# Output products of 512 columns for ten of sixteen granules, with the halves added by VectorE

## The chip, the core and the metric

The kernel runs on one core of one Trainium2 chip. The metric is the device time of one launch in microseconds. A comparison uses the median of several runs; the profile is one further execution, recorded by the hardware profiler.

## What is computed

The output is `x + A(xn) + B(xn)`, where `xn` is the layer norm of `x` (2048 tokens of 1024 columns, bfloat16). `A` is attention with a recurrent memory: the tokens are cut into 64 segments of 32, and each segment attends over itself and 8 memory rows that the segment before it produced.

```
for s in range(n_seg):                       # 64 segments, one after another
    h = concat([mem, x[s]])                  # 8 memory rows + 32 tokens
    q, k, v = h @ Wq, h @ Wk, h @ Wv         # 32 heads of 128
    p = softmax(mask(q k^T * scale))
    o = (p v) @ Wo                           # 40 rows of 1024
    mem, out[s] = o[:8], o[8:]
```

`B` picks the two tokens with the highest router score, sends them through a gated feed-forward network and adds the result to these two rows. It makes up the last part of the program and is not touched.

## The kernel before, in words

**Main rows and left rows.** The memory of a segment depends on the segment before it, so the segments are a strict sequence. Of a segment's 32 tokens, the first 24 ("main" rows) go with the 8 memory rows as 32 rows through the products of that segment. The last 8 tokens ("left" rows) of four segments are gathered into another 32 rows per group of four segments (`G, j = divmod(s, 4)`), whose products (`left_pass` at L579, `project_left` at L598) are spread over the group as fillers, at places written out by hand in `PASSES`.

**Granules.** The four weight matrices are cut into 64 granules of 128 partitions x 2048 columns (512 KB). Granules 0 to 47 are Wq, Wk and Wv in six phases of eight (`PHASES`), granules 48 to 63 are Wo, each with the rows of two heads: an even head in its columns 0 to 1023, an odd one in 1024 to 2047. 44 granules stay in SBUF. The other 20 (`STREAMED`) are loaded in each segment again, by SyncE (`fetch`, L366), from a copy in DRAM (`wsc`) into five slots (`N_SLOT`). A slot's next load is issued as soon as TensorE has done with its granule (`after`, called by `release`). Granule 6 is kept whole in PSUM instead, and of granule 25 a half. The kept pieces of granule 6 are copied back to SBUF once in a segment by `bring_back` (L389): pieces 1 and 2 after output granule 9, piece 1 by ScalarE and piece 2 by VectorE; pieces 3 and 0 at the beginning of the next segment.

**Phases.** In each of the phases 0 to 5 of a segment a granule makes four products of 512 columns (L817): the stationary operand is a chunk of 32 columns of `ST` (the normalized main rows and the memory rows, transposed), and the four products go to the four groups of 32 partitions of one PSUM bank. The sums are copied out, transposed and used for scores, softmax and attention by functions that `hook` places at a phase and granule.

**The output stage** (called phase 6) takes the 16 granules of Wo. `project` (L586) makes for each of a granule's two heads four products of 256 columns, product `g` with the columns `256 g` and on to partitions `32 g` to `32 g + 31`, columns 0 to 255 of the bank `WO`. Columns 256 to 415 of the same bank hold sums of the attention of half 0 until ScalarE has copied them (L745, L747). Attention of half 1 is called ahead of granules 5 and 8 (`attend(1, 0)`, `attend(1, 1)`); its results are copied by ScalarE (first product group) and VectorE (second), to `OT` for the main rows and `OTL` for the left rows. After granule 15 VectorE adds `WO` to `X[s % 2]`, the residual rows in the same layout (L885), POOL sends out the rows (L887), and the memory rows are transposed into the next segment's `ST` (`mem_to_st`: L301 on TensorE, L324 on VectorE). With these the next segment's phase 0 can begin. `run_passes(7, 0)` and `run_passes(8, 0)` put left passes of TensorE into that gap.

**Names that matter for the change.** `psA` has two PSUM banks with the tag "acc", for the six `PSm` of a segment and for `WO`, in turn. `roles` is a list of three SBUF tags of 1024 bytes per partition that rotates once in a group; `roles[0]` is the one that is free for short tenants: `XBl` (sums of the left rows' q and k, copied by `copy_unit` at L627 and stored to `ql_d` by a DMA that ScalarE issues, L628), `BX` and `XL` (left rows and zeros), and piece 0 of granule 6 (`BK`). In segments 1 and 2 of a group the second of two such stores is issued behind the copy of phase 5's sums (L846). A tile that takes over a tag waits until everything that used the tile before it is done, its DMAs too. Every engine works off its instructions in order.

**Order of columns.** `X`, the memory rows and the output use blocks of 256 columns, block `g` on partitions `32 g`. The left rows' output already uses products of 512 columns and the crossed order `2 * (g % 2) + g // 2`, and adds its halves in `copy_unit` (L616, L619).

Of the kernel before, what the change touches and what calls it, by code (L numbers as in the profile page):

```python
# [9 lines left out]
F32 = mybir.dt.float32  # L10
U32 = mybir.dt.uint32
ALU = mybir.AluOpType
# [4 lines left out]

N_RES = 44
N_SLOT = 5
KEPT_WHOLE = 6  # L20
KEPT_PART = 25
NEG = -30000.0
# [28 lines left out]
def kernel(  # L51
# [16 lines left out]
    nc = tc.nc  # L68
# [204 lines left out]
    def two_rows(m, tag):  # L273
# [52 lines left out]
    def load_left(G, t, crossed=False):  # L326

        o4 = x2[4 * G * SEG:4 * (G + 1) * SEG, :].rearrange("(s r) d -> s r d", s=4)[:, XM:SEG, :]
        if not crossed:
            o4 = o4.rearrange("s r d -> r s d")  # L330
        for g in range(4):
            b = 2 * (g % 2) + g // 2 if crossed else g
            nc.gpsimd.dma_start(out=t[32 * g:32 * (g + 1), :], in_=o4[:, :, 256 * b:256 * (b + 1)])
        return t

# [33 lines left out]
    def part(t, jq):  # L369
        return t[jq][:, :] if isinstance(t, list) else t[:, 512 * jq:512 * (jq + 1)]  # L370
# [16 lines left out]
    def bring_back(c, copy):  # L387
        back[c] = one.tile([P, 512], BF16, tag=(roles[0], "bE", "kt", "bC")[c], name="BK")
        copy(out=back[c][:, :], in_=KEPT_COLS[KEPT_WHOLE][c])  # L389

# [45 lines left out]
    OB = one.tile([P, 256], BF16, tag="bA", name="MEM0")  # L436
    nc.vector.memset(OB[:, :], 0.0)
    for g in range(4):
        nc.gpsimd.dma_start(out=OB[32 * g + XM:32 * g + SEG, :], in_=A_mem0[0, :, 256 * g:256 * (g + 1)])
    n_x = 1  # L440
    n_q = 0
    for g in range(48):
# [99 lines left out]
    def passes_of(s):  # L542
        out = {}
        for at, ps in places[s % 4].items():
            for u, g in ps:
                if not 0 <= group_of(u, s) < NT:
                    continue
                if s == 0:
                    after_first.append((u, g))
                elif s == NSEG - 1 and u == "o":  # L550
                    pass
                else:
                    out.setdefault(at, []).append((u, g))
        if s == 1:
            out.setdefault((0, 7), []).extend(after_first)
        if s == NSEG - 1:
            for w in range(16):
                out.setdefault((6, max(w, 3)), []).append(("o", 48 + w))
        return out
# [19 lines left out]
            nc.tensor.matmul(PSl[32 * jq:32 * jq + 32, :], lhsT=STL[:, g % KC, :], rhs=part(Gv, jq),  # L579
                             start=first_, stop=last_, tile_position=(0, 32 * jq))  # L580

    def project(PS, w, Gv, lhs, last, first=False):
        for hs in range(2):
            h = 2 * w + hs
            for g in range(4):
                nc.tensor.matmul(PS[32 * g:32 * g + 32, 0:256], lhsT=lhs(h),  # L586
                                 rhs=Gv[:, D * hs + 256 * g:D * hs + 256 * (g + 1)], start=(first and hs == 0),
                                 stop=(last and hs == 1), tile_position=(0, 32 * g), skip_group_check=True)

    xl_of, otl_of = [None], [None]  # L590

# [9 lines left out]
    def copy_unit(u, s, engine):  # L601
        PS, n = units.pop(u)
        assert n == 0, (u, s, n)
        Gu = group_of(u, s)
        copy = nc.scalar.copy if engine == "scalar" else nc.vector.tensor_copy
        half = int(u[-1]) if u != "o" else 0
        if u[0] == "v":
            new_vl[half] = one.tile([P, 512], BF16, tag=roles[half], name="VL")
            copy(out=new_vl[half][:, :], in_=PS[:, :])
            if half:  # L610
                roles.insert(0, roles.pop())
        elif u == "o":
            OL = xl_of[0]
            LF = one.tile([P, 256], F32, tag="otl", name="LF")
            for c in range(2):
                nc.scalar.copy(out=LF[64 * c:64 * c + 64, :], in_=PS[64 - 64 * c:128 - 64 * c, 256 * c:256 * c + 256])  # L616
            for c in range(2):
                here = slice(64 * c, 64 * c + 64)
                nc.vector.tensor_tensor(out=LF[here, :], in0=PS[here, 256 * c:256 * c + 256], in1=LF[here, :], op=ALU.add)  # L619
            nc.gpsimd.tensor_tensor(out=OL[:, :], in0=LF[:, :], in1=OL[:, :], op=ALU.add)  # L620
            o4 = out2[4 * Gu * SEG:4 * (Gu + 1) * SEG, :].rearrange("(s r) d -> s r d", s=4)
            for g in range(4):
                b = 2 * (g % 2) + g // 2
                nc.gpsimd.dma_start(out=o4[:, XM:SEG, 256 * b:256 * (b + 1)], in_=OL[32 * g:32 * (g + 1), :])
        else:
            XBl = one.tile([P, 512], BF16, tag=roles[0], name="XBl")
            copy(out=XBl[:, :], in_=PS[:, :])  # L627
            stores.append(lambda: nc.scalar.dma_start(out=ql_d[Gu][2 * half + "qk".index(u[0])], in_=XBl[:, :]))  # L628
            if engine == "scalar":
                stores.pop()()  # L630

    for s in range(NSEG):
# [91 lines left out]
        def attend(half, ph, turn_too=None):  # L724
            if half not in sums:
                if half not in OT:
                    OT[half] = one.tile([P, 4, 4, SEG], BF16, tag=("kt", "bC")[half], name="OT")
                if half == 0:
                    nxt["wo"] = psA.tile([P, 512], F32, tag="acc", name="WO")
                sums[half] = [BS[:, 0:4 * NK] if half else nxt["wo"][:, 256:256 + 4 * NK], OPB]  # L730
            PTm, PTl = PTs[half]
            for il in range(4):
                for jl in range(2):
                    q0 = 32 * (2 * ph + jl)
                    o = sums[half][jl][:, il * NK:(il + 1) * NK]
                    nc.tensor.matmul(o, lhsT=VM[half][q0:q0 + 32, il * P:(il + 1) * P], rhs=PTm[q0:q0 + 32, il, 0:NK],  # L736
                                     start=True, stop=False, tile_position=(q0, 0), skip_group_check=True)
                    nc.tensor.matmul(o, lhsT=VL[half][q0:q0 + 32, il * P:(il + 1) * P], rhs=PTl[q0:q0 + 32, il, 0:NK],
                                     start=False, stop=True, tile_position=(q0, 0), skip_group_check=True)
            if turn_too is not None:  # L740
                turn_too()
            for jl in range(2):
                ov = sums[half][jl].rearrange("p (i q) -> p i q", i=4)
                copy = nc.scalar.copy if half == 0 or jl == 0 else nc.vector.tensor_copy
                copy(out=OT[half][:, 2 * ph + jl, :, :], in_=ov[:, :, 0:SEG])  # L745
                h0 = 16 * half + 8 * ph + 4 * jl
                copy(out=left_out()[:, h0:h0 + 4, j, :], in_=ov[:, :, SEG:NK])  # L747
# [61 lines left out]
        for p, (mat, half) in enumerate(PHASES):  # L809
# [3 lines left out]
            for kc in range(KC):  # L813
                g = 8 * p + kc
                Gv = back if s > 0 and g == KEPT_WHOLE else granule(g)
                for jq in range(4):
                    nc.tensor.matmul(PSm[32 * jq:32 * jq + 32, :], lhsT=ST[:, kc, :], rhs=part(Gv, jq),  # L817
                                     start=(kc == 0), stop=(kc == KC - 1), tile_position=(0, 32 * jq))
                if g in KEPT_COLS and s == 0:
                    keep(g, Gv)  # L820
                if s > 0:
                    held[g] = Gv
                    run_passes(p, kc)
                    release(p, kc)
                else:
                    behind.append((g, Gv))
                    if kc >= 3 or p == 0:
                        for g_, Gv_ in behind:
                            left_pass(PSl, g_, Gv_, g_ % KC == 0, g_ % KC == KC - 1)
                            after(s, g_)  # L830
                        behind = []
                for fn in hooks.pop((p, kc), []):
                    fn()
# [30 lines left out]
        for w in range(16):  # L864
# [18 lines left out]
            release(6, w)  # L883
        OB = X[s % 2]
        nc.vector.tensor_tensor(out=OB[:, :], in0=WO[:, 0:256], in1=OB[:, :], op=ALU.add)  # L885
        for g in range(4):
            nc.gpsimd.dma_start(out=out2[s * SEG:s * SEG + XM, 256 * g:256 * (g + 1)], in_=OB[32 * g:32 * g + XM, :])  # L887
        run_passes(7, 0)
        if s + 1 < NSEG:
            mem_to_st(OB, nxt["st"])  # L890
# [123 lines left out]
```

## Time and profile before

| | |
|---|---|
| median of 3 runs | 1869.23 us (1857.4 to 1875.79) |
| time of the profiled execution | 1871.21 us |
| its span, first to last instruction | 1869.1 us |
| mean granted TensorE clock | 0.957 |
| TensorE products of L586 | 8192 matmuls, 8192 weight loads |
| TensorE products of L817 | 12288 matmuls |
| bytes moved by DMA | 712.27 MB, 381 GB/s in the mean |

How to read the profile: PE is TensorE's matmuls, PEld its weight loads, DVE VectorE, ACT ScalarE, POOL GpSimd, SP SyncE. A line of the groups names the kernel line, the engine, the operation, the tile written and those read, the shape, the count, the busy time, the mean duration in ns, and the idle time of the engine just ahead of it with what ended that. In the order of time a row begins with its start and its length in us; a count behind it says how many instructions follow each other in it, and brackets give the idle time ahead. In the chain of waits each row is a start, a length and what the chain passes through. A table by stage gives for each engine busy time and count, then the granted clock, the share of the 16 DMA engines and GB/s. The last row of an answer on one line gives its DMAs' time from issue to landing.

### The profile page before, as it was taken

How to read it: one execution, taken by the hardware profiler on the slowest of the kernel's cores; microseconds unless marked ns; L12 is line 12 of the kernel's file. 1: busy time of each engine (PE TensorE's matmuls, PEld its weight loads, DVE VectorE, ACT ScalarE, POOL GpSimd, SP SyncE). 2: the span in 40 equal slices, each digit the busy share in tenths (PEclk: the TensorE clock that was granted, in tenths of full speed). 3: DMA queues.
4: the chain of work that ended last, by engine and by line, in shares of the span. 5: the costliest groups of instructions: out<-in, count | busy, mean ns of one | idle time of the engine just before them, and what ended most of it. 6: DMA issues, size and time to landing. Idle time of an engine off the chain costs nothing.

```text
span 1869.1 us, 80529 instructions
## 1 busy us (share of the span) xinstructions
PE 1568.8 (84%) x34978; PEld 847.9 (45%) x34978; DVE 896.9 (48%) x2950; ACT 683.6 (37%) x1933; POOL 457.1 (24%) x898
## 2 busy tenths in 40 slices
PE   3458998898998988888899988988889988988764
PEld 1124444444444444444444444444445544444433
DVE  6725544554455444544554455544544455445430
ACT  1113433444343433434344334434334343433320
POOL 3111322213231322223132322323132221312220
PEclk8669999999999999999999999999999999999995
DMA  9999999999999999999999999999999999999998
GB/s 370 406 355 373 388 386 380 393 382 387 394 385 392 366 383 391 359 380 385 388 375 388 389 384 387 373 396 374 378 369 396 394 382 383 378 377 352 384 402 338
DMA packets 230322, 712.27 MB, mean 381 GB/s; under 512 B 39040, under 2 KB 52912, under 8 KB 229968
## 3 DMA queue, kind: packets, MB, share of 16 engines
q1 hardware_dynamic: 192592, 671.18, 93.0%
q0 software_dynamic: 28736, 28.08, 4.7%
q10 hardware_dynamic: 8640, 7.87, 1.2%
q8 instruction: 274, 4.49, 0.9%
q14 instruction: 80, 0.66, 0.1%
HBM read 694.32 MB, written 22.29 MB: 383 GB/s over the span
## 4 chain that ended last, share of the span: by engine, by line
DMA 61%; PE 32%; DVE 4%; issue 1%; ACT 1%; SPq 0%; ACTq 0%; DVEq 0%
DMA g<-wsc 54%; PE PSm L817 17%; PE WO L586 4%; PE PSl L579 4%; PE BT L649 2%; DMA XP<-in_A_x_dram 2%; PE WL L598 1%; DMA MW<-in_B_w_gate_dram 1%; DVE XR L256 1%; DMA MW<-in_B_w_up_dram 1%; DMA g<-in_A_Wq_dram 1%; DMA wres<-in_A_Wo_dram 1%; DMA g<-in_A_Wo_dram 1%; DMA MW<-in_B_w_down_dram 1%; DMA g<-in_B_w_down_dram 1%
## 5 line engine op out<-in xcount | busy, mean ns | idle before, releaser
L817 PE MATMUL PSm<-wres,ST 128*32 128x512 bf16 x8448 | 700.5, 383 | 6.5 <-DMA wres<-in_A_Wv_dram 3.5
L817 PEld LDWEIGHTS <-ST 128*32 128x32 bf16 x12288 | 323.6, 96 | 412.7 <-issue 168.2
L817 PE MATMUL PSm<-g,ST 128*32 128x512 bf16 x3588 | 360.0, 386 | 97.7 <-DMA g<-wsc 76.3
L586 PEld LDWEIGHTS <-OT 128*32 128x32 bf16 x8192 | 217.6, 97 | 166.6 <-issue 141.0
L836 ACT CAST XB<-PSm 128x512 bf16<-128x512 f32 x256 | 150.7, 589 | 283.9 <-PE PSm L817 280.8
L586 PE MATMUL WO<-wres,OT 128*32 128x256 bf16 x5632 | 237.6, 278 | 12.3 <-DMA wres<-in_A_Wo_dram 8.0
L495 POOL DMA_DIRECT2D LX<-ql_d x63 | 35.4, 562 | 814.0 <-PE WO L586 423.2
L586 PE MATMUL WO<-g,OT 128*32 128x256 bf16 x2560 | 133.3, 281 | 84.1 <-DMA g<-wsc 72.6
L579 PE MATMUL PSl<-wres,STL 128*32 128x512 bf16 x2112 | 184.5, 390 | 0.4 <-issue 0.4
L887 POOL DMA_DIRECT2D out_dram<-X x256 | 130.2, 515 | 211.9 <-DVE X L885 169.4
L664 DVE COPY KT<-BT 128x512 bf16<-128x512 bf16 x112 | 45.9, 410 | 278.7 <-issue 121.8
L281 POOL DMA_DIRECT2D X<-in_A_x_dram x256 | 130.1, 515 | 179.6 <-PE PSm L817 88.8
L389 ACT COPY BK<-KEPT 128x512 bf16<-128x512 bf16 x126 | 74.3, 590 | 131.2 <-PE WO L586 99.8
L657 ACT COPY QT<-BT 128x512 bf16<-128x512 bf16 x128 | 75.0, 586 | 127.1 <-PE BT L502 78.1
L649 PEld LDWEIGHTS <-XB 128*128 128x128 bf16 x1024 | 58.6, 98 | 117.1 <-ACT XB L836 75.2
L885 DVE TENSOR_TENSOR X<-WO,X 128x256 bf16<-128x256 f32 x64 | 27.2, 425 | 172.3 <-PE WO L586 172.3
L649 PE MATMUL BT<-IDENT,XB 128*128 128x128 bf16 x1024 | 102.2, 223 | 8.2 <-ACT XB L836 6.7
L579 PEld LDWEIGHTS <-STL 128*32 128x32 bf16 x3072 | 84.0, 98 | 53.0 <-issue 8.5
L846 ACT CAST VM<-PSm 128x512 bf16<-128x512 f32 x128 | 76.5, 598 | 83.3 <-PE PSm L817 82.8
L736 PEld LDWEIGHTS <-VM 32*128 32x128 bf16 x2048 | 65.1, 91 | 83.7 <-issue 72.7
L393 DVE COPY g<-KEPT 128x512 bf16<-128x512 bf16 x126 | 47.6, 420 | 101.7 <-PE PSm L817 51.5
L681 DVE TENSOR_TENSOR BS<-BS,CT 128x96 f32<-128x96 f32 (+1 forms) x256 | 59.1, 231 | 72.8 <-PE BS L674 68.3
(175 smaller groups left out, 2371.9 us busy)
## 6 DMA issues: line engine op xcount, KB each, us to landing
g<-wsc SPq DMA_DIRECT2D x1134, 512.0 KB, 6.0
g<-wsc SPq DMA_DIRECT2D x63, 256.0 KB, 5.7
LX<-ql_d POOLq DMA_DIRECT2D x63, 128.0 KB, 5.6
ql_d<-XBl ACTq DMA_DIRECT2D x60, 128.0 KB, 5.8
MW<-in_B_w_gate_dram SPq DMA_DIRECT2D x16, 448.0 KB, 9.5
MW<-in_B_w_up_dram SPq DMA_DIRECT2D x16, 448.0 KB, 9.1
wres<-in_A_Wk_dram SPq DMA_DIRECT2D x12, 512.0 KB, 11.9
MW<-in_B_w_down_dram SPq DMA_DIRECT2D x12, 512.0 KB, 10.1
```

The lines of the kernel that those rows point to most:

```text
L281: nc.gpsimd.dma_start(out=X[s % 2][32 * g:32 * g + XM, :], in_=x2[s * SEG:s * SEG + XM, 256 * g:256 * (g + 1)])
L389: copy(out=back[c][:, :], in_=KEPT_COLS[KEPT_WHOLE][c])
L579: nc.tensor.matmul(PSl[32 * jq:32 * jq + 32, :], lhsT=STL[:, g % KC, :], rhs=part(Gv, jq), start=first_, stop=last_, tile_position=(0, 32 ...
L586: nc.tensor.matmul(PS[32 * g:32 * g + 32, 0:256], lhsT=lhs(h), rhs=Gv[:, D * hs + 256 * g:D * hs + 256 * (g + 1)], start=(first and hs == ...
L649: nc.tensor.transpose(out=PTq[:, il, :, :].rearrange("p j r -> p (j r)"), in_=XB[:, il * P:(il + 1) * P], identity=IDENT[:, :])
L657: nc.scalar.copy(out=QT[half][:, :, :], in_=pv)
L681: nc.vector.tensor_tensor(out=S4, in0=S4, in1=m, op=ALU.add)
L736: nc.tensor.matmul(o, lhsT=VM[half][q0:q0 + 32, il * P:(il + 1) * P], rhs=PTm[q0:q0 + 32, il, 0:NK], start=True, stop=False, tile_position ...
L817: nc.tensor.matmul(PSm[32 * jq:32 * jq + 32, :], lhsT=ST[:, kc, :], rhs=part(Gv, jq), start=(kc == 0), stop=(kc == KC - 1), tile_position= ...
L836: nc.scalar.copy(out=XB[:, :], in_=PSm[:, :])
L846: nc.scalar.copy(out=VM[half][:, :], in_=PSm[:, :])
L887: nc.gpsimd.dma_start(out=out2[s * SEG:s * SEG + XM, 256 * g:256 * (g + 1)], in_=OB[32 * g:32 * g + XM, :])
```

## The change

- In output granules 0 to 9 (`N_WIDE`) each head makes two products of 512 columns in place of four of 256. The even head's go to partitions 0 to 63, the odd head's to 64 to 127, so that after granule 9 the bank holds two halves of the sum.
- Ahead of granule 10 `add_halves` adds them with four VectorE operations on 64 partitions x 256 columns into a new float32 tile `SUM` (tag `roles[0]`): first the one half and the residual rows `X`, then the other half. Granules 10 to 15 go, in products of 256 columns as before, to a second `WO` bank from `psA`. The final add takes `SUM` in place of `X`.
- The blocks of 256 columns are in the crossed order throughout: in the loads of `X` and the first memory, in the output, and in the choice of the chunk of `ST` at L817. The transfers keep their number and size.
- The last attention copies (`half == 1`, `jl == 1`, `ph == 1`) and piece 2 of granule 6 are copied by ScalarE in place of VectorE.
- The left passes of segment 0 that are placed in the gap at its end (`at[0]` of 7 or 8) stay there; before, they were all put off to segment 1.

```diff
+N_WIDE = 10
+    def block(g):
+        return 2 * (g % 2) + g // 2
...
-                                in_=x2[s * SEG:s * SEG + XM, 256 * g:256 * (g + 1)])
+                                in_=x2[s * SEG:s * SEG + XM, 256 * block(g):256 * (block(g) + 1)])
...
-                if s == 0:
+                if s == 0 and at[0] < 7:
                     after_first.append((u, g))
...
-    def project(PS, w, Gv, lhs, last, first=False):
+    def project(PS, w, Gv, lhs):
         for hs in range(2):
             h = 2 * w + hs
+            if w < N_WIDE:
+                for c in range(2):
+                    r0 = 64 * hs + 32 * c
+                    nc.tensor.matmul(PS[r0:r0 + 32, :], lhsT=lhs(h), rhs=Gv[:, D * hs + 512 * c:D * hs + 512 * (c + 1)],
+                                     start=(w == 0), stop=(w == N_WIDE - 1), tile_position=(0, r0), skip_group_check=True)
+                continue
             for g in range(4):
                 nc.tensor.matmul(PS[32 * g:32 * g + 32, 0:256], lhsT=lhs(h),
-                                 rhs=Gv[:, D * hs + 256 * g:D * hs + 256 * (g + 1)], start=(first and hs == 0),
-                                 stop=(last and hs == 1), tile_position=(0, 32 * g), skip_group_check=True)
+                                 rhs=Gv[:, D * hs + 256 * block(g):D * hs + 256 * (block(g) + 1)],
+                                 start=(w == N_WIDE and hs == 0), stop=(w == 15 and hs == 1), tile_position=(0, 32 * g),
+                                 skip_group_check=True)
+
+    def add_halves(PS, src, mid, dst):
+        for out, a, flip in ((mid, src, True), (dst, mid, False)):
+            for c in range(2):
+                here = slice(64 * c, 64 * c + 64)
+                there = slice(64 - 64 * c, 128 - 64 * c) if flip else here
+                nc.vector.tensor_tensor(out=out[here, :], in0=PS[there, 256 * c:256 * c + 256], in1=a[here, :], op=ALU.add)
...
-                copy = nc.scalar.copy if half == 0 or jl == 0 else nc.vector.tensor_copy
+                copy = nc.scalar.copy if half == 0 or jl == 0 or ph == 1 else nc.vector.tensor_copy
...
-                    nc.tensor.matmul(PSm[32 * jq:32 * jq + 32, :], lhsT=ST[:, kc, :], rhs=part(Gv, jq),
+                    nc.tensor.matmul(PSm[32 * jq:32 * jq + 32, :], lhsT=ST[:, 2 * block(kc // 2) + kc % 2, :], rhs=part(Gv, jq),
...
             Gv = granule(48 + w)
-            project(WO, w, Gv, lhs_main, w == 15, first=(w == 0))
+            if w == N_WIDE:
+                SUM = one.tile([P, 256], F32, tag=roles[0], name="SUM")
+                add_halves(WO, X[s % 2], SUM, SUM)
+                WO = psA.tile([P, 512], F32, tag="acc", name="WO")
+            project(WO, w, Gv, lhs_main)
...
                 bring_back(1, nc.scalar.copy)
-                bring_back(2, nc.vector.tensor_copy)
+                bring_back(2, nc.scalar.copy)
...
-        nc.vector.tensor_tensor(out=OB[:, :], in0=WO[:, 0:256], in1=OB[:, :], op=ALU.add)
+        nc.vector.tensor_tensor(out=OB[:, :], in0=WO[:, 0:256], in1=SUM[:, :], op=ALU.add)
```

The same `block(g)` stands in for `g` in the load of the first memory and in the output transfers.

More of the change, by code (lines that the diff above doesn't have):

```diff
@@ L438 @@
     for g in range(4):
-        nc.gpsimd.dma_start(out=OB[32 * g + XM:32 * g + SEG, :], in_=A_mem0[0, :, 256 * g:256 * (g + 1)])
+        nc.gpsimd.dma_start(out=OB[32 * g + XM:32 * g + SEG, :], in_=A_mem0[0, :, 256 * block(g):256 * (block(g) + 1)])
     n_x = 1
@@ L884 @@
         OB = X[s % 2]
-        nc.vector.tensor_tensor(out=OB[:, :], in0=WO[:, 0:256], in1=OB[:, :], op=ALU.add)
+        nc.vector.tensor_tensor(out=OB[:, :], in0=WO[:, 0:256], in1=SUM[:, :], op=ALU.add)
         for g in range(4):
-            nc.gpsimd.dma_start(out=out2[s * SEG:s * SEG + XM, 256 * g:256 * (g + 1)], in_=OB[32 * g:32 * g + XM, :])
+            nc.gpsimd.dma_start(out=out2[s * SEG:s * SEG + XM, 256 * block(g):256 * (block(g) + 1)], in_=OB[32 * g:32 * g + XM, :])
         run_passes(7, 0)
```

4 lines of the change are left out of this document (2 added, 2 removed).

## The prediction

> **What bounds the kernel now.** I read the page from its first part to the chain, then a table by stage, then the order of time around one segment boundary.
>
> ```profile
> span 1869.1 us, 80529 instructions
> PE 1568.8 (84%) x34978; PEld 847.9 (45%) x34978; DVE 896.9 (48%) x2950; ACT 683.6 (37%) x1933; POOL 457.1 (24%) x898
> DMA  9999999999999999999999999999999999999998
> DMA packets 230322, 712.27 MB, mean 381 GB/s; under 512 B 39040, under 2 KB 52912, under 8 KB 229968
> q8 instruction: 274, 4.49, 0.9%
> DMA 61%; PE 32%; DVE 4%; issue 1%; ACT 1%; SPq 0%; ACTq 0%; DVEq 0%
> L817 PE MATMUL PSm<-g,ST 128*32 128x512 bf16 x3588 | 360.0, 386 | 97.7 <-DMA g<-wsc 76.3
> L586 PE MATMUL WO<-g,OT 128*32 128x256 bf16 x2560 | 133.3, 281 | 84.1 <-DMA g<-wsc 72.6
> ```
>
> The DMA engines are busy nine tenths or more in every slice but the last, 61% of the chain is DMA, and TensorE, busy 84%, stands waiting for a streamed granule for 76.3 + 72.6 us, some 2.4 us in each of the 63 segments that stream. By stage:
>
> ```profile
> 400.00:600.00 200.00, 182.22 (x4112) 97.27 (x4104) 100.61 (x337) 81.97 (x233) 52.86 (x103) 1.00 1.02 390
> 600.00:800.00 200.00, 176.19 (x3961) 95.89 (x3954) 93.83 (x319) 76.48 (x219) 51.90 (x101) 0.97 0.99 374
> 1200.00:1400.00 200.00, 175.98 (x3994) 94.33 (x3994) 95.87 (x320) 78.93 (x220) 50.66 (x99) 1.00 1.00 378
> ```
>
> The last three columns are the granted clock, the DMA share and GB/s. The share is 0.99 to 1.02 throughout and the clock is full, so what is left to win is the spread between 374 and 390 GB/s: all 712.27 MB at 390 would take 1826 us. The change moves no byte of data more or less. TensorE still matters, because it frees the five stream slots, and the chain shows where it takes over:
>
> ```profile
> 896.98 6.77 DMA g<-wsc
> 903.79 0.62 PE WO L586 x16
> 904.41 0.65 PE PSl L579 x12
> 905.05 0.22 PE BT L301 x2
> 913.90 6.44 DMA g<-wsc
> ```
>
> Here the chain leaves a transfer at 903.75, crosses the segment boundary on TensorE and enters the next transfer at 913.90. So a late boundary can cost time, if the transfer queue has no reserve.
>
> **The change part by part.** The terms use this stretch, the end of an output stage with a store pending, and the same point one segment later:
>
> ```profile
> 896.70 0.19 ACT L747 CAST OTL<-WO 128x32 bf16<-128x32 f32 x1
> 896.94 0.62 PE L586 MATMUL WO<-wres,OT 128*32 128x256 bf16 x16
> 897.82 0.33 ACTq L628 DMA_DIRECT2D ql_d<-XBl  x1
> 899.76 0.40 PE L586 MATMUL WO<-g,OT 128*32 128x256 bf16 x8
> 899.97 0.62 PE L586 MATMUL WO<-wres,OT 128*32 128x256 bf16 x16
> 901.09 0.19 ACT L747 CAST OTL<-BS 128x32 bf16<-128x32 f32 x1
> 901.27 0.61 PE L586 MATMUL WO<-wres,OT 128*32 128x256 bf16 x16
> 901.46 0.41 DVE L389 COPY BK<-KEPT 128x512 bf16<-128x512 bf16 x1
> 901.63 0.32 ACT L315 COPY ST<-BT 128x192 bf16<-128x192 bf16 x1 [0.35 <-DVE OTL L747]
> 903.79 0.40 PE L586 MATMUL WO<-g,OT 128*32 128x256 bf16 x8 [0.57 <-DMA g<-wsc]
> 904.46 0.42 DVE L885 TENSOR_TENSOR X<-WO,X 128x256 bf16<-128x256 f32 x1 [2.58 <-PE WO L586]
> 904.50 0.59 ACT L389 COPY BK<-KEPT 128x512 bf16<-128x512 bf16 x1 [2.06 <-PE WO L586]
> 905.65 0.60 PE L817 MATMUL PSm<-wres,ST 128*32 128x512 bf16 x8
> 906.08 0.39 PE L817 MATMUL PSm<-g,ST 128*32 128x512 bf16 x4
> 924.30 0.33 ACTq L628 DMA_DIRECT2D ql_d<-XBl  x1
> 931.20 0.42 DVE L885 TENSOR_TENSOR X<-WO,X 128x256 bf16<-128x256 f32 x1 [3.67 <-PE WO L586]
> ```
>
> 1. **Wide products.** Ten granules of a segment go from eight products of 256 columns to four of 512; over 64 segments 2560 matmuls and 2560 weight loads go. TensorE time: eight of 256 columns start at 899.76 and the next granule at 899.97, 0.21 us; eight of 512 (two granules) run from 905.65 to 906.08, 0.43 us, 0.215 per granule. The column groups already run four at a time, so a granule costs the same: 0, with bounds of 0.005 us either way on 640 granules, 3 us of TensorE time.
>
> The Trainium skill ("TensorE: Matmul & The Clock Gate", Back-to-back issue gap) says that in a stream of weight load and matmul pairs a matmul of 128 columns takes about 81 ns and one of 512 about 131 ns, which would make 256 columns some 98 ns (an estimate between its two figures) and a granule 784 against 524 ns. The trace, with 26 ns per product of 256 and 54 per product of 512, does not agree, and it decides.
>
> 2. **Instruction fetch.** 5120 of 80529 instructions go. Queue 8 moves 4.49 MB of instructions at 0.9% of 16 engines; 5120/80529 of 0.9% of 1869.1 us is 1.1 us less transfer time. If the loads and products of TensorE alone make this queue (69956 for 274 packets), 20 packets go.
>
> 3. **Adding the halves.** Four additions on 64 partitions. The nearest rows are the same operation in the left rows' path:
>
> ```profile
> L619 DVE TENSOR_TENSOR LF<-WL,LF x32: 409/422/428, 224.6 to 1812.2; 64x256 f32<-64x256 f32 x32
> 1811.80 0.85 DVE L619 TENSOR_TENSOR LF<-WL,LF 64x256 f32<-64x256 f32 x2
> ```
>
> Two in 0.85 us, so four take 1.70 us. They can begin when granule 9 of the stage is done, about 901.75 in this stretch, and end at 903.45, ahead of the final add at 904.46, in time VectorE waited out (2.58 us). In the quickest boundaries granule 9 and the end lie closer, and a tenth or two of a microsecond may show: 0 to 3 us in all, I take 0.
>
> 4. **The place of SUM.** It takes the slot that the rotating role 0 names, and that slot's last tenant decides. In segments 1 and 2 of each group this is the XBl that VectorE filled in phase 5 and that ScalarE then sends out:
>
> ```profile
> L627 DVE CAST XBl<-PSl x30: 650/652/692, 151.1 to 1668.5; 128x512 bf16<-128x512 f32 x30
> L628 ACTq DMA_DIRECT2D ql_d<-XBl x60: 325/327/361, 136.9 to 1669.2; - x60
> DMA to landing us min/median/max: 4.2/5.8/7.4
> L389 DVEq EVENT_SEMAPHORE  x30: 21/21/21, 159.6 to 1676.6; - x30
> ```
>
> Today the next tenant is BK, copied at 905.49 in the following segment, and its 30 waits take 21 ns each: the store has long landed. After the change the first addition asks four microseconds sooner. Issued at 897.82, landed 5.8 us later at 903.62, additions to 905.32: the final add, at 904.46 now, comes 0.86 us late. One segment later: 924.30, 930.10, 931.80 against 931.20, 0.60 late. Mean 0.73 us in 30 segments, 22 us of later boundaries. With the shortest landing (4.2) there is no delay, with the longest (7.4) 2.3 us, which over 30 would be 70, but no trace has them all long. Behind the waiting addition stand, on VectorE, the final add and then the memory columns of ST; for these wait the transposes of L301, all products of the next phase 0, and POOL's four output transfers.
>
> How much of the 22 us reaches the end? The same line for the stream's loads (L366) says little of it:
>
> ```profile
> DMA to landing us min/median/max: 3.3/6.0/10.3
> ```
>
> 3.3 us at the least, 6.0 in the median: a typical transfer stands 2.7 us in the queue and one issued 0.73 us later mostly lands when it would have. Against that stands the chain above, which crosses this boundary on TensorE. Bounds 0 and 22; nearer the reserve I take a fifth, **+5 us**.
>
> 5. **Copies given to ScalarE.** The last attention copies and the kept piece (0.41 us on VectorE, 0.59 on ScalarE) join a queue that had 2.06 us free before 904.50. ST's copy at 901.63 waited 0.35 us for VectorE's OTL; with two copies of about 0.28 and 0.2 us ahead of it, behind the 901.09 row's end, it starts near 901.76, 0.13 later; its reader comes after 904.46. The last heads' OT is first needed by the granule at 903.79. 0 us; without that cover some 0.1 us a segment, 8 us.
>
> 6. **Banks.** Wide products fill the columns where attention's sums lie. They must wait for the copy that ends at 896.89, and the narrow ones start at 896.94 already: no new wait. The second WO takes the bank of phase 5, copied before 897.7 and wanted at 901.7; the next phase 0 takes the first WO's bank, which the additions leave ahead of the final add. 0.
>
> 7. **Column blocks and the first segment.** The transfers keep number and size: 0. Five granules' left passes (5 x 0.215 = 1.1 us of TensorE) move from segment 1 to the end of segment 0: between -1.1 and +1.1, taken as 0.
>
> Sum: 1871.2 us of the profiled execution - 1.1 + 5 = 1875. That execution lies 2.0 us over the median of the runs, 1869.2, so the forecast is **1873 us**, no change that could be measured. About 1%, 19 us, is what a measurement of this kernel can tell from none: its three runs alone lie between 1857.4 and 1875.8.
>
> **The rivals.**
>
> *Slower: the store's landing sets every second boundary.* The 22 us come through whole if the stream's queue is empty when TensorE resumes. For it: the chain crosses the boundary on TensorE. Against it: the 2.7 us of queue and 2.4 us of waiting per segment in which TensorE can catch up. Time 1869 + 22 - 1 = 1890 us. It decides from the point where the final add is later than the queue's reserve, or the reserve is under about 0.7 us.
>
> *Faster: instruction packets hold up the stream.* A packet of queue 8 takes one DMA engine for 0.009 x 16 x 1869.1 / 274 = 0.98 us, and a granule has landed only when all engines have brought their part. If every such packet delayed the stream fully, 20 fewer would be worth 20 us: 1849 us. Against it: 274 x 0.98 = 269 us of such stalls would show as a DMA share far under 0.99.
>
> *Faster: weight loads in the open.* If the 40 loads fewer in a segment, 97 ns each, were not hidden, 64 x 40 x 0.097 = 248 us of TensorE time would go, and the stream would run at its best stretch, 1826 us. The equal spacing of item 1 speaks against it. The skill's page named there would have it so in part, with 0.26 us saved on each of 640 granules.
>
> ```profile
> L586 PEld LDWEIGHTS <-OT 128*32 128x32 bf16 x8192 | 217.6, 97 | 166.6 <-issue 141.0
> ```
>
> **How the numbers follow.** Forecast 0.78, the late boundary in full 0.13, instruction packets 0.06, weight loads 0.03. Within 1% (1850.5 to 1888) therefore 0.78, slower by more 0.13, faster by more 0.09. The range runs from 1854 (the fetch term at nearly its full price) to 1892 (the late boundary in full, with a microsecond or two of items 3 and 5): 1854 to 1892.
>
> **What would show it.** Right: the wide line with 2560 matmuls, granules 0.21 us apart; queue 8 near 254 packets; in 30 segments the first addition released by the DMA of ql_d and the final add 0.5 to 1 us later; a shorter wait of TensorE for g<-wsc by about as much; the same GB/s. Wrong: the GB/s of the stages beyond 374 to 390, TensorE's waits for g<-wsc unchanged while boundaries are later, additions that wait for nothing, or ST's copy on the chain.

## The result and the profile after

Six runs of the changed kernel have a median of **1911.48 us** (1909.65 to 1917.85), six of the kernel before 1868.37 us (1857.4 to 1875.79). The ratio is **1.0245 [1.0209, 1.0281]**: the change costs some 46 us, where the prediction had no change that could be measured, and a range that ended at 1892. Of the executions below two, 1933.05 and 2067.45 us of experiment 7, are slow ones (the second with a granted clock of 0.729), and every ratio is formed without them.

The page of the changed kernel, in the lines that answer to those of before:

```profile
span 1916.1 us, 75793 instructions
PE 1570.1 (82%) x32418; PEld 783.2 (41%) x32418; DVE 958.9 (50%) x3015; ACT 727.3 (38%) x2124; POOL 457.3 (24%) x898
DMA packets 230306, 711.97 MB, mean 372 GB/s; under 512 B 39040, under 2 KB 52912, under 8 KB 229968
q8 instruction: 254, 4.16, 0.8%
DMA 50%; PE 35%; DVE 11%; issue 2%; ACT 1%; SPq 1%; POOL 0%; DVEq 0%; ACTq 0%; POOLq 0%
```

TensorE's busy time is 1570.1 us against 1568.8, with 2560 matmuls fewer. Practically the same bytes take 47 us longer, at 372 GB/s against 381. On the chain VectorE has risen from 4 to 11%: VectorE did not become a busy engine (50%), but something of it now stands between two pieces of the path. The waits say what. The first row is of the kernel before, the other two are of the kernel after; behind a releaser stand the sum in us, the number of waits and the longest.

```profile
PEld L301 <- DVE X L885: 29.0, 62, 1.2
```

```profile
DVE SUM L606 <- DMA ql_d<-XBl: 121.3, 29, 5.5
PEld L305 <- DVE X L907: 75.7, 63, 3.4
```

In 29 boundaries the first addition waits for the store of `XBl`. TensorE, at the head of the next segment, waits for the final add 75.7 us in all against 29.0. Two such boundaries follow each other on the chain of waits of the changed kernel:

```profile
922.24 5.56 DMA ql_d<-XBl
...
927.89 0.43 DVE SUM L606
...
929.25 0.44 DVE SUM L606
...
929.78 0.43 DVE X L907
930.21 0.05 issue
930.26 0.29 PE BT L305 x2
...
949.34 5.69 DMA ql_d<-XBl
...
955.12 0.42 DVE SUM L606
...
957.01 0.44 DVE X L907
```

Store, four additions, final add, the transposes of the next segment: each begins where the one before ends, and from 922.24 to 930.55 nothing else is on the path. Before, the chain crossed such a boundary on TensorE. From the store's issue to the final add it is 7.54 us in the first of these boundaries and 7.67 in the second. Over all 30 such pairs of rows the mean is 8.09 us, against 6.61 in the kernel before (its pairs in the prediction: 904.46 - 897.82 = 6.64 and 931.20 - 924.30 = 6.90). So the final add comes **1.47 us late** in 30 boundaries, 44 us.

That TensorE was ready earlier is seen in the order of time at the second boundary:

```profile
955.12 0.87 DVE L606 TENSOR_TENSOR SUM<-WO,X 64x256 f32<-64x256 f32 x2 [3.96 <-DMA ql_d<-XBl]
955.38 0.40 PE L596 MATMUL WO<-wres,OT 128*32 128x256 bf16 x8
955.60 0.83 PE L583 MATMUL PSl<-wres,STL 128*32 128x512 bf16 x12
957.01 0.42 DVE L907 TENSOR_TENSOR X<-WO,SUM 128x256 bf16<-128x256 f32 x1
957.49 0.29 PE L305 MATMUL BT<-IDENT,X 128*128 128x128 bf16 x2 [1.05 <-DVE X L907]
```

The last products of the segment run while the first addition does. The additions end 1.1 us after these products, and after 12 products of a left pass TensorE stands for another 1.05 us.

The stages show what the stream makes of it:

```profile
400.00:600.00 200.00, 173.09 (x3600) 85.49 (x3594) 102.56 (x331) 81.87 (x245) 49.85 (x96) 0.98 0.98 368
600.00:800.00 200.00, 174.46 (x3683) 87.87 (x3680) 101.09 (x323) 84.09 (x245) 53.39 (x104) 1.00 0.99 378
1200.00:1400.00 200.00, 169.81 (x3562) 85.12 (x3561) 100.54 (x319) 80.67 (x239) 51.46 (x100) 0.99 0.99 369
```

368 to 378 GB/s where 374 to 390 had been, and still a DMA share of 0.98 and 0.99.

The loss sits behind the late boundaries. Take the last load that is issued ahead of a final add and the first one behind it. Over the 28 boundaries of segments 1 and 2 in groups 1 to 14 these two are 4.06 us apart in the mean, where they are 2.36 us apart in the kernel before: for 1.7 us more no slot comes free. From 2 to 10 us after the start of the final add the DMA engines then move 296 GB/s in the mean, against 368 before, and from 10 to 16 us 388 against 386. One boundary near the mean, that of segment 1 in group 8, first in the kernel after (final add at 1040.06), then in the kernel before (at 1009.85):

```profile
1042.00:1050.00 8.00, 8.00 (x172) 3.96 (x164) 2.62 (x8) 3.62 (x7) 3.05 (x7) 1.00 0.94 291
```

```profile
1011.80:1019.80 8.00, 7.54 (x160) 3.65 (x152) 1.78 (x6) 3.52 (x7) 3.04 (x7) 1.00 1.00 363
```

The first of the two boundaries on the chain above has the shortest distance of all 28, 2.74 us, and shows no such stretch (388 GB/s from 2 to 10 us behind its final add). So while TensorE waits it frees no slot, no load is issued, and some microseconds later the stream runs thin. This is the hole, and no faster stretch behind it fills it.

### The profile page after: what moved, and what is told of

Read it like the earlier page. It is cut to its first block, busy times and chain, and to the rows that moved or that the text cites. A ratio compares the mean times of both kernels' runs of the same rounds, so it can differ in the third digit from the quotient of the medians.

```text
span 1916.1 us, 75793 instructions
## 1 busy us (share of the span) xinstructions
PE 1570.1 (82%) x32418; PEld 783.2 (41%) x32418; DVE 958.9 (50%) x3015; ACT 727.3 (38%) x2124; POOL 457.3 (24%) x898
## 4 chain that ended last, share of the span: by engine, by line
DMA 50%; PE 35%; DVE 11%; issue 2%; ACT 1%; SPq 1%; POOL 0%; DVEq 0%; ACTq 0%; POOLq 0%
DMA g<-wsc 34%; PE PSm L835 20%; DMA ql_d<-XBl 9%; PE PSl L583 5%; DVE SUM L606 3%; PE BT L667 2%; PE WO L592 2%; DMA XP<-in_A_x_dram 2%; PE WL L616 1%; DMA MW<-in_B_w_gate_dram 1%; DMA g<-in_A_Wq_dram 1%; DVE XR L257 1%; DMA MW<-in_B_w_up_dram 1%; PE BT L305 1%; DMA wres<-in_A_Wo_dram 1%
## 5 line engine op out<-in xcount | busy, mean ns | idle before, releaser
L835 PE MATMUL PSm<-g,ST 128*32 128x512 bf16 x3588 | 363.3, 390 | 99.1 <-DMA g<-wsc 76.8
L592 PE MATMUL WO<-wres,OT 128*32 128x512 bf16 x1792 | 150.5, 388 | 10.3 <-DMA wres<-in_A_Wo_dram 9.3
L606 DVE TENSOR_TENSOR SUM<-WO,X 64x256 f32<-64x256 f32 x128 | 54.0, 422 | 193.9 <-DMA ql_d<-XBl 121.3
L393 ACT COPY BK<-KEPT 128x512 bf16<-128x512 bf16 x189 | 108.3, 628 | 109.3 <-PE WO L596 109.3
L596 PEld LDWEIGHTS <-OT 128*32 128x32 bf16 x3072 | 84.1, 97 | 94.1 <-issue 76.2
L592 PEld LDWEIGHTS <-OT 128*32 128x32 bf16 x2560 | 66.9, 95 | 106.9 <-issue 71.7
L864 ACT CAST VM<-PSm 128x512 bf16<-128x512 f32 x128 | 76.8, 600 | 79.9 <-PE PSm L835 79.6
L592 PE MATMUL WO<-g,OT 128*32 128x512 bf16 x768 | 78.4, 395 | 33.1 <-DMA g<-wsc 28.2
```

What stands on the lines that cost most here:

```text
L592: nc.tensor.matmul(PS[r0:r0 + 32, :], lhsT=lhs(h), rhs=Gv[:, D * hs + 512 * c:D * hs + 512 * (c + 1)], start=(w == 0), stop=(w == N_WIDE - ...
L606: nc.vector.tensor_tensor(out=out[here, :], in0=PS[there, 256 * c:256 * c + 256], in1=a[here, :], op=ALU.add)
L835: nc.tensor.matmul(PSm[32 * jq:32 * jq + 32, :], lhsT=ST[:, 2 * block(kc // 2) + kc % 2, :], rhs=part(Gv, jq), start=(kc == 0), stop=(kc = ...
L864: nc.scalar.copy(out=VM[half][:, :], in_=PSm[:, :])
```

## The experiments

**Theory.** `SUM`'s place is the whole cause: the additions wait for the store, the boundary is late, and a late boundary passes to the end nearly in full. **Rivals.** The additions, the wide products or the moved copies cost something themselves. The stream has a reserve that takes up short delays, so that 1.5 us hurts only because it is beyond it. A delay hung on a store costs more than one of fixed length, since the store itself is issued later after each late segment.

**1. SUM in a place without a store** (`e1_sum_elsewhere`). `SUM` goes to the slot `bE`, which no store uses at that point. Piece 0 of granule 6, needed later, goes to `bE` too, and piece 1, which ScalarE copies, to the rotating slot. All else of the change stays.

```diff
-        back[c] = one.tile([P, 512], BF16, tag=(roles[0], "bE", "kt", "bC")[c], name="BK")
+        back[c] = one.tile([P, 512], BF16, tag=("bE", roles[0], "kt", "bC")[c], name="BK")
...
-                SUM = one.tile([P, 256], F32, tag=roles[0], name="SUM")
+                SUM = one.tile([P, 256], F32, tag="bE", name="SUM")
```

The two `bring_back` calls after granule 9 also change their order.

> The changed kernel, with SUM in the slot bE, which nothing with a pending store uses at that point; piece 1 of granule 6 goes to the rotating slot instead (copied by ScalarE, after piece 2), and piece 0 to bE. Nothing is left out of the computation. Theory (the 29 waits of the first addition for the DMA of ql_d are the whole loss): the 121 us of VectorE waiting for that DMA go, the final add follows the last product within 0.1 us in all segments, and the time is that of before, 1868 us within 10. Rival (the loss is in the other parts: wide products, additions, copies moved to ScalarE): the time stays near 1911, above 1895 in any case.

Measured: 1863.62 us, **0.9956 [0.9932, 0.998]**. The first additions wait for products alone, and the wait of TensorE is back at its old size; the first row is from the answer on the additions' line, the second from the waits.

```profile
  PE WO L592: 115.3, 64
```

```profile
PEld L305 <- DVE X L907: 29.9, 63, 0.9
```

The store still has somebody waiting for it: ScalarE, with the copy of piece 1, for 66.6 us in 30 waits (`ACT BK L393 <- DMA ql_d<-XBl`). But with VectorE's wait gone the same change costs nothing and gains 0.2 to 0.7%. From the store's issue to the final add it is 6.36 us in the mean here, with the additions in: they lie in VectorE's free time as forecast.

**2. No new tile at all** (`e2_sum_in_x`). The sums are rounded to bfloat16 in the residual tile, `SUM` is gone.

```diff
-                SUM = one.tile([P, 256], F32, tag=roles[0], name="SUM")
-                add_halves(WO, X[s % 2], SUM, SUM)
+                SUM = X[s % 2]
+                add_halves(WO, SUM, SUM, SUM)
```

> The changed kernel without the tile SUM: the additions are made in place in X, so the sums are rounded to bfloat16 twice more; everything else is as in the change. It takes the wait away in another way than the run before, with no slot exchanged and ScalarE's order kept. Theory (the wait alone): 1868 us within 10, as the run before. Rival (the other parts cost): above 1895. If this run and the one before differ by over 10 us, the exchange of slots itself has a price.

Measured: 1861.88 us, 0.9973 [0.9953, 0.9992], TensorE's wait 29.3 us in 63. It is a second way out with the same answer, so it was the place and not something else about piece 0 or the tag bE.

**3 and 4. A late boundary alone** (`e3_late_add_2`, `e4_late_add_4`). The kernel before, with two or four reductions of `WO` into an unused tile ahead of the final add, in segments 1 and 2 of each group (32 boundaries). It has no wide products, no `SUM` and no waiting for a store.

```diff
+        if j in (1, 2):
+            DL = one.tile([P, 8], F32, tag="nm", name="DL")
+            for i in range(2):
+                nc.vector.tensor_reduce(out=DL[:, i:i + 1], in_=WO[:, 0:256], axis=AX.X, op=ALU.add)
```

> The kernel before the change, with two VectorE reductions of WO (128 x 256, some 0.42 us each) ahead of the final add in segments 1 and 2 of each group, 32 segments: the final add is about 0.85 us late there, and nothing else differs. Theory (a late boundary passes on to the end in full): 32 x 0.85 = 27 us, 1895 us. Rival (the queue's reserve of 2.7 us takes it up, as the prediction had it): at most a fifth, 5 us, 1868 to 1874 us.

> As the run before with four reductions, about 1.7 us late in 32 segments, close to the 1.5 us that the profile of the change shows in its late segments. Theory (passed on in full): 54 us, 1923 us, and twice the price of the run before. Rival (a reserve that empties at some point): less than a fifth up to about 1 us, then steep, so under 1885 us and far more than twice the price of the run before.

Measured: two give 1879.27 us, 1.0076 [1.0031, 1.012]; four give 1902.63 us, 1.0165 [1.0135, 1.0195]. The wait rows of the two kernels, one fence each:

```profile
PEld L301 <- DVE X L889: 46.5, 61, 1.5
```

```profile
PEld L301 <- DVE X L889: 67.0, 62, 2.1
```

Both times lie between what the full price and the reserve had led me to expect, in part because the reductions add less than their own length to TensorE's wait: 17.5 and 38.0 us over the 29.0 of before, where 64 and 128 of them take 24.2 and 45.4 us by the groups. Set against that wait, the price is 14 / 17.5 and 31 / 38.0, 0.8 us of time for each. As far as the intervals reach, the first half microsecond per boundary costs as much as the second. At the lower end of its interval (0.3%, 6 us) the kernel with two reductions still pays 0.18 us for each of its 32 boundaries, of 0.55 us of added wait, so a reserve could take up at most 0.37 us (an estimate from these figures). The reserve of 2.7 us that I had relied on falls; a small one isn't excluded.

**5 and 6. The wait alone, ahead of the additions or behind them** (`e5_wait_ahead_of_adds`, `e6_wait_behind_adds`). To experiment 2 one memset of a single column of a tile in `roles[0]` is added in segments 1 and 2: it waits for the same store and does next to nothing. For the first it stands as here, for the second behind `add_halves`.

```diff
+                if j in (1, 2):
+                    WAITED = one.tile([P, 256], F32, tag=roles[0], name="WAITED")
+                    nc.vector.memset(WAITED[:, 0:1], 0.0)
                 add_halves(WO, SUM, SUM, SUM)
```

> The run with the sums in X, and the wait put back by itself: in segments 1 and 2 of each group VectorE clears one column of a tile in the rotating slot, right ahead of the four additions, so it waits there for the store of XBl as the changed kernel did. Theory (that wait is the whole loss): 1910 us within 8, the final add 1.5 us late in 30 segments. Rival (it was SUM's float32 form or its reads that cost): the time stays near 1862.

> As the run before, but the clearing stands behind the four additions, so that these are done in the free time and only the clearing and the final add follow the landing. Theory (the 1.9 us of additions queued behind a landing that itself comes near the last product are what makes the boundary late): late by 0.2 to 0.4 us in the mean, 1862 to 1876 us. Rival (any wait of VectorE for that store costs what it cost in the change, wherever it stands): above 1900.

Measured: ahead, 1918.05 us, **1.0269 [1.0221, 1.0317]**; behind, 1866.35 us, **0.9978 [0.9952, 1.0005]**. Waits of the first and of the second:

```profile
DVE WAITED L896 <- DMA ql_d<-XBl: 122.5, 30, 6.2
PEld L305 <- DVE X L910: 78.6, 63, 4.6
```

```profile
DVE WAITED L897 <- DMA ql_d<-XBl: 25.4, 26, 2.9
PEld L305 <- DVE X L910: 36.3, 63, 2.9
```

This is the sharpest pair. The instructions are the same and so is the store; only what is queued behind the wait differs. Behind the additions the wait is nearly over when VectorE comes to it (25.4 us in 26 waits), and what follows, the final add, is hardly later. Ahead of them, 1.9 us of work is queued behind the landing. So, as in experiment 1, the price was not that of waiting for a store but of the four additions standing **behind** it.

**7 and 9. A fixed delay of the same length, with wide products** (`e7_fixed_late_5`, `e9_fixed_late_5_again`). Experiment 1 with five reductions ahead of the final add in segments 1 and 2: a boundary as late as the changed kernel's, and not hung on the store.

```diff
+        if j in (1, 2):
+            DL = one.tile([P, 8], F32, tag="nm", name="DL")
+            for i in range(5):
+                nc.vector.tensor_reduce(out=DL[:, i:i + 1], in_=WO[:, 0:256], axis=AX.X, op=ALU.add)
```

> The kernel with SUM in bE and five reductions of WO ahead of the final add in 32 segments, so a boundary that is late by a fixed 1.7 us, about the change's 1.5, but counted from the last product and not from the store. Theory A (a late boundary costs what its length says, however it came about): 32 x 1.7 x 0.8 to 1.0 = 44 to 54 us over 1864, 1907 to 1918. Theory B (the change lost more because its final add hangs on the store, whose own time hangs on the boundary before, so that a late boundary can't be made good in the output stage; a fixed delay can): the slope of the two fixed delays, 0.8 beyond the first 0.7 us, gives some 38 us, 1898 to 1905.

Inconclusive: of 1917.61, 1933.05, 2067.45 and 1900.41 us two are left, and they lie too far apart for a ratio. So it was measured once more with more runs.

> The same kernel as the fixed delay of five reductions (1.7 us in 32 segments, SUM in bE), with more rounds, since its four times lay 1900 to 1933 us and one far off. Theory A (a late boundary costs what its length says): 1907 to 1918 us. Theory B (a fixed delay is partly made good, only one that hangs on the store is not): 1898 to 1905.

Measured: 1915.17 us, 1.0252 [1.0217, 1.0288], with

```profile
PEld L305 <- DVE X L911: 83.6, 63, 2.6
```

From the store's issue to the final add it is 8.14 us here in the mean, 8.09 in the changed kernel, and the ratios are 1.0252 and 1.0245. A delay of fixed length costs what the one hung on the store costs. The rival of a worse price for a store falls, as far as the intervals reach (some 0.5%, 9 us).

**8. The copies alone** (`e8_copies_only`). The kernel before, with the last attention copies and piece 2 copied by ScalarE and segment 0's passes left in their gap.

```diff
-                if s == 0:
+                if s == 0 and at[0] < 7:
...
-                copy = nc.scalar.copy if half == 0 or jl == 0 else nc.vector.tensor_copy
+                copy = nc.scalar.copy if half == 0 or jl == 0 or ph == 1 else nc.vector.tensor_copy
...
-                bring_back(2, nc.vector.tensor_copy)
+                bring_back(2, nc.scalar.copy)
```

> The kernel before with the small parts alone: the last attention copies and piece 2 by ScalarE, and segment 0's left passes kept at its end; no wide products, no additions. The two kernels without the wait came out 4 to 8 us under before. Theory (the wide products, by fewer instructions to fetch, give that): the time is that of before, 1868 within 4. Rival (VectorE's relief or the moved passes give it): 1860 to 1864.

Measured: 1870.42 us, 0.9997 [0.9973, 1.0022]. The copies of item 5 and the moved passes of item 7 are worth nothing within 0.3%, as put, and so they are not shown to give the small gain of experiments 1 and 2; up to 5 us of it the interval leaves open.

**10. One late boundary per group in place of two** (`e10_wait_segment_1`). Experiment 5 with `if j == 1`.

> The run with the wait put back ahead of the additions, but in segment 1 of each group only: 15 waits of the first addition for the store in place of 30. Theory A (each late boundary costs its 1.5 to 1.9 us): half of the price of both, 1862 + 28 = 1890 us. Theory B (the price comes from two late boundaries in a row, the second hanging on the first): clearly under half, 1868 to 1880.

Measured: 1894.62 us, 1.0163 [1.0112, 1.0213].

```profile
DVE WAITED L896 <- DMA ql_d<-XBl: 67.6, 15, 5.6
PEld L305 <- DVE X L910: 53.4, 62, 3.0
```

Half the waits (15 for 30), half the added wait of TensorE (24.1 of 49.3 us) and, over experiment 2, 35 of 55 us of time. A single late boundary is not absorbed by the three that follow it, so it does not take a second one in a row to do damage. That it seems to cost a little more than half is within the interval of about 10 us.

**11. Is there a reserve in the queue?** (`e11_four_slots`). The prediction had read one from the landing time, 6.0 us in the median and 3.3 at the least. If 2.7 us of that were waiting in a queue, one slot fewer should shorten the queue and not the kernel.

```diff
-N_SLOT = 5
+N_SLOT = 4
```

> The kernel before with four stream slots in place of five; nothing else. It asks whether the stream has a reserve at all. The prediction's reading (DMA engines busy throughout, 2.7 us of queue in the median landing): a slot less takes 1.4 us of the queue away and costs little, under 1885 us. Rival (the stream goes round a loop of five slots, release by TensorE, landing 6 us later, so that what delays a release delays the stream): four slots carry clearly less, above 1920 us.

Measured: 2077.2 us, **1.1107 [1.1061, 1.1153]**. The page, the page's group, the line of the loads and one stage:

```profile
DMA packets 230322, 712.27 MB, mean 342 GB/s; under 512 B 39040, under 2 KB 52912, under 8 KB 229968
L817 PE MATMUL PSm<-g,ST 128*32 128x512 bf16 x3588 | 362.8, 391 | 214.9 <-DMA g<-wsc 198.3
```

```profile
DMA to landing us min/median/max: 3.3/5.5/7.8
```

```profile
600.00:800.00 200.00, 162.78 (x3584) 88.34 (x3580) 83.79 (x278) 69.39 (x195) 41.67 (x83) 0.97 0.95 341
```

The median falls by 0.5 us only, and the kernel takes 11% longer. So the 6 us is mostly the load's own time with five of them under way, and no queue that a late issue could be taken from. The same numbers as a round of one slot: a segment of 26.5 us (924.30 - 897.82) has 19 loads (1197 over 63 segments), 1.39 us each; with five slots one slot's round is 7.0 us, of which 6.0 go to the landing and the remaining 1.0 to all that lies between a landing and the slot's next issue (waiting for TensorE, its products, the signals). With four slots a segment is (2077.2 - 1869.8) / 63 = 3.3 us longer, 1.57 us per load, a round of 6.3 us: 5.5 and 0.8. The rest is got by difference, so the two sides agree by construction and show nothing alone. What shows it is that one slot fewer shortens the landing by 0.5 us, where a mere queue would give up one load's 1.39 us, and costs 11%. Release, issue, landing and release form a loop with little slack: a TensorE that stands for a microsecond longer lengthens every round under way, and little wins it back. And the DMA share of 0.95 at 341 GB/s shows that a share near one does not mean that the engines are at their rate.

**The price of a late boundary.** Each row is the added wait of TensorE for the final add against the added time (from the ratios, times 1869 us).

| kernel, against | boundaries | added wait, us | added time, us | time per wait |
|---|---|---|---|---|
| two reductions, before | 32 | 17.5 | 14 | 0.8 |
| four reductions, before | 32 | 38.0 | 31 | 0.8 |
| five reductions (9), experiment 1 | 32 | 53.7 | 55 | 1.0 |
| the change, experiment 1 | 30 | 45.8 | 54 | 1.2 |
| wait ahead (5), experiment 2 | 30 | 49.3 | 55 | 1.1 |
| wait in segment 1 (10), experiment 2 | 15 | 24.1 | 35 | 1.5 |

Each time is uncertain by 5 to 10 us, so the differences between 0.8 and 1.2 are not settled. That the price is near one, and not near the prediction's fifth, is. Taken instead by how much later the final add follows the store's issue (0.40, 1.00, 1.78, 1.73 and 1.93 us a boundary in the first five rows), the price is 0.95 to 1.1. The segments themselves say it too: between final adds, segments 1 and 2 (of groups 1 to 14) take 27.99 and 28.37 us in the mean in the changed kernel, 26.36 and 26.56 in experiment 1. That is 1.6 and 1.8 us more, for a final add that comes 8.09 - 6.36 = 1.73 us later after the store. Segment 3 gives 0.46 us back (25.55 against 26.01), and segment 0 none (27.69 against 27.59).

**What stays open.** Experiments 1 and 2 are 0.4 and 0.3% faster than the kernel before, with intervals that just leave out no change. The copies and the moved passes showed no gain in experiment 8. The wide products with their additions remain, with TensorE's instruction packets in them, and these were not tried apart. Experiment 1 is the version that beats both kernels.

## Why the prediction was wrong, point by point

- **Wide products (item 1): right.** Two granules of four products each start at 927.03, 927.26 and the next follows at 927.48, 0.22 us a granule as with eight of 256 columns:

```profile
927.03 0.40 PE L592 MATMUL WO<-g,OT 128*32 128x512 bf16 x4
927.26 0.39 PE L592 MATMUL WO<-wres,OT 128*32 128x512 bf16 x4
927.48 0.39 PE L596 MATMUL WO<-wres,OT 128*32 128x256 bf16 x8
```

- **Instruction fetch (item 2): right.** Queue 8 went from 274 to 254 packets, the 20 foreseen. The rival by which each packet holds up the stream (-20 us) gets at most the gain of experiments 1 and 2, 5 to 8 us (13 at the far end of the interval).
- **Additions (item 3): right where no store is pending.** They take 1.89 us to the final add's start (927.89 to 929.78), 0.19 more than put, and cost nothing in experiment 1.
- **SUM's slot (item 4): the mechanism was right and two sizes were wrong.** The step that failed is "nearer the reserve I take a fifth". The 2.7 us between the shortest and the median landing were taken for a queue; experiment 11 shows that they are not one, and experiments 3, 4 and 9 that a boundary's delay costs 0.8 to 1.0 us for each us of wait. The second is the lateness itself, 0.73 us from a single stretch, against 1.47 in the mean of 30. Of the difference, 0.19 are the longer additions, 0.16 the stretch (6.77 us from store to final add, where the mean is 6.61), and 0.09 the time from the landing to the first addition (927.80 to 927.89); the remaining 0.3 is what landings longer than the median add: 8.09 - 1.89 - 0.09 leaves 6.1 us for the landing in the mean, where 5.8 was put. With both sizes as measured the item is 30 x 1.47 x about 1.0 = 44 us, and the sum 1869 + 44 - 1 = 1912, where 1911 was measured. That it meets so closely is in part chance: against experiment 1, which has all of the change but VectorE's wait, the late boundaries cost 54 us (30 x 1.73 are 52), and the rest of the change gains some 8.
- **Copies (5) and moved passes (7): right**, by experiment 8. The column blocks of item 7 are in experiments 1 and 2 only and cost nothing there. **Banks (6): right**: the last copy and the first wide products stand as close as the narrow ones did.

```profile
920.68 0.19 ACT L765 CAST OTL<-WO 128x32 bf16<-128x32 f32 x1
920.92 0.62 PE L592 MATMUL WO<-wres,OT 128*32 128x512 bf16 x8
```

- **The slower rival had the place, the mechanism and its sign**, at 1890 us and a chance of 0.13. Its own point of decision, a reserve "under about 0.7 us", was met (at most 0.37 us, by experiment 3). What the prediction held against it, 2.4 us of waiting per segment "in which TensorE can catch up", is where the argument went wrong: that wait is part of the loop. TensorE can only catch up with loads that have landed, and behind a late TensorE these are issued late, 4.06 us after the last one where it was 2.36.
- **What would show it.** 29 first additions released by the store (30 were named), a final add later by more than the 0.5 to 1 us, and GB/s out of the band: three signs in the direction of the rival. The shorter wait for g<-wsc did not come, which was to say that nothing is made up. It is 76.8 us for the phases (76.3 before) and 28.2 + 50.5 for the two kinds of output products (72.6 before):

```profile
L835 PE MATMUL PSm<-g,ST 128*32 128x512 bf16 x3588 | 363.3, 390 | 99.1 <-DMA g<-wsc 76.8 <-DMA g<-in_A_Wq_dram 13.1 <-DMA g<-in_A_Wv_dram 5.1
L592 PE MATMUL WO<-g,OT 128*32 128x512 bf16 x768 | 78.4, 395 | 33.1 <-DMA g<-wsc 28.2 <-DMA g<-in_A_Wo_dram 2.4
L596 PE MATMUL WO<-g,OT 128*32 128x256 bf16 x1024 | 52.1, 279 | 54.8 <-DMA g<-wsc 50.5 <-DMA g<-in_A_Wo_dram 3.7
```

## What to carry to other kernels

A tile that takes over a buffer inherits the last reader's transfer. Look up when that lands, and what work stands behind the wait on its engine: a wait of VectorE for the same store cost 2.7% ahead of 1.9 us of additions and nothing measurable behind them. Where buffers are freed by the engine that the transfers feed, a landing time that is long against its minimum is no proof of a reserve. Take one buffer away, or delay the freeing engine by a known length: here the first cost 11%, and a delay counted at about its own length. Take a delay's size from all its occurrences, not from one stretch.

## What the hardware showed that was not expected

After a wait of TensorE of 1.81 us the granted clock was 0.50 for some three microseconds, and a wide granule took twice its time: two of them run in 0.62 us at 920.92 but in 1.09 us at 923.74.

```profile
923.30:926.30 3.00, 2.94 (x40) 0.94 (x39) 0.44 (x3) 0.36 (x2) 0.00 (x0) 0.50 1.01 392
```

```profile
923.36 0.62 PE L592 MATMUL WO<-g,OT 128*32 128x512 bf16 x4 [1.81 <-DMA g<-wsc]
923.74 1.09 PE L592 MATMUL WO<-wres,OT 128*32 128x512 bf16 x8
```

So here a wait was followed by a few microseconds at half of TensorE's speed. Between the first and the last final add the stretches at 0.50 add up to 47.8 us in the changed kernel's profiled run, 20.5 in that of the kernel before, 17.1 in experiment 1 and 34.1 in experiment 9. Half of what each has more than experiment 1, 15 and 9 us, is an estimate of the most that the clock itself can have cost of the 54 and 55 us. That is a part of the price of a late boundary and not the main part; these are single executions, and no run here keeps the clock up to tell more.
